# Two attention blocks on one core: the first x and K loads copied plain and transposed by TensorE

## The chip, the cores and the metric

One core of one Trainium2 chip. The metric is the device time of one execution in microseconds; lower is better. Before the change it is 1212.87 us, the median of three runs (1212.12 to 1215.04).

## What is computed

Two independent attention blocks, A and B, of the same shape, whose outputs stand side by side in the last dimension:

```python
# x 16x144x448, k_cache and v_cache 16x16x512x256, wq 448x4096, wo 4096x448, all bf16
q = (x @ wq).reshape(B, Sq, H, Dh).transpose(0, 2, 1, 3)
scores = jnp.einsum("bhqd,bhkd->bhqk", q, k_cache) * (Dh ** -0.5)
p = softmax(scores, axis=-1)
o = jnp.einsum("bhqk,bhkd->bhqd", p, v_cache)
out = o.transpose(0, 2, 1, 3).reshape(B, Sq, H * Dh) @ wo
# result: concatenate([out of A, out of B], axis=-1), 16x144x896
```

## The kernel before

The work is cut into 512 **units** (`NT`): 2 blocks x 16 batches x 16 heads, A first. A unit is 144 query rows against 512 keys of depth 256. Line numbers are those of the profile.

Every buffer is allocated by hand, and the program of each engine is written by one loop over **slots** `i`. In a slot each step is emitted for the unit that is due there: Q for unit `i + LQ` (15 ahead), SA for `i + LS` (5 ahead), TA for `i + LT` (2 ahead), PV for `i`. A small bookkeeper (`_Sched.add`) turns the reads and writes of each step into semaphore waits; each engine then executes its own list strictly in order. Nothing is reordered at run time.

The steps of a unit:

- **Q** (`t_q`, L316): 8 matmuls 128x144 into the one bank `qp_ps`; evacuated with the factor 1/16 into `qt_sb` by VectorE (L328) or ScalarE (L332).
- **SA** (`t_sa`, L424): scores of the first 112 query rows, 2 matmuls 128x512 into one of two banks `sa_ps`; then maximum on VectorE (L436), exponential on ScalarE (L447), reciprocal on VectorE (L457), normalisation on GpSimd (L465).
- **SB** (`t_sb`, L348): scores of the last 32 rows of 8 units together, 16 matmuls into two banks `sb_ps`; once in 8 slots, in slot 8n - 7 for group n. It needs the whole K block of the group and the Q of its 8 units.
- **TA** and **TB** (L478, L401): the probabilities transposed by TensorE, 4 transposes each, evacuated by VectorE (L488, L410).
- **PV** (`t_pv`, L511): 8 matmuls into one of two banks `ot_ps`; evacuated by ScalarE (L526) into a ring that collects batches.
- **OP** (`t_op_piece`, L549): output projection of finished chunks of 128 rows with `wo`, in pieces of 2 matmuls between the other steps, from slot 17 on. Evacuated at L567 (ScalarE) or L570 (VectorE), and stored by GpSimd's queue (`t_store`, L578). The last two chunks end in the banks `op_ps` and `qp_ps`.

**Loads.** All go through SP's queue, in an order that is sorted beforehand by deadline (`plan`: a deadline, an earliest slot `lo` and a lead). x comes for four batches at a time by two DMA transposes (L281, L282; `xt_sb`, three buffers). K comes for 8 units at a time by one DMA transpose (L291; `kt_sb`, three buffers): K0 is the block of units 0 to 7, K1 of 8 to 15, and so on. V comes for 4 units at a time as a plain copy (L301; `v_sb`, three buffers; V0 for units 0 to 3). wq comes in four parts for four heads each, two copies a part (L260, L262): wq0 for units 0 to 3, and so on. wo comes in 8 parts of 448 KB (L270). A load into a buffer waits on SP for the last reader of what lay there.

The order on SP's queue at the start of the kernel before is x, wq0, wq1, wq2, K0, wq3, V0, K1, V1, V2, K2, wo, V3, 2 wo, V4, K3, 2 wo, V5, 2 wo, V6, K4, wo, V7, V8, K5.

Of the kernel before, what the change touches and what calls it, by code (L numbers as in the profile page):

```python
# [122 lines left out]
def bass_concat_heads__mha_block_cached__gqa_block_cached__near_ridge_kernel(  # L123
# [52 lines left out]
    with contextlib.ExitStack() as es:  # L176
# [126 lines left out]

        def t_q(U):
# [4 lines left out]
            hg = h // 4  # L309

            def e(t):
                ins = None
                for kc in range(4):
                    for dc in range(2):
                        c0 = h * DH + dc * 128
                        ins = t.matmul(qp_ps[:, dc * SQ:(dc + 1) * SQ], lhsT=wq_sb[:, kc, c0:c0 + 128],  # L316
# [3 lines left out]
            S.add(PE, e, reads=[(("wq", hg), pr), ("wqz", 0), (("xt", xsl), XG)], writes=[("qp", ("q", U))],  # L320
                  banks=["qp"], name="Q%d" % U)

        def t_evac_q(U):
            sl = U % NQT
            src = qp_ps[:, 0:2 * SQ].rearrange("p (c q) -> p c q", c=2)
            if (U - LQ) % 8 in (2, 4, 6, 7):
                def e(v):
                    return v.tensor_scalar(qt_sb[:, sl, :, :], src, 1.0 / 16.0, None, op0=ALU.mult)  # L328
                S.add(DVE, e, reads=[("qp", ("q", U))], writes=[(("qt", sl), U)], banks=["qp"], name="eq%d" % U)
            else:  # L330
                def e(a):
                    return a.activation(qt_sb[:, sl, :, :], src, AF.Copy, scale=1.0 / 16.0)  # L332
# [240 lines left out]
        def t_store(r):  # L573
            pr, row0, m = chunk_rows(r)
            sl = r % NOST

            def e(q):
                return q.dma_start(of[row0:row0 + m, pr * D:(pr + 1) * D], ost_sb[0:m, sl, :]).then_inc(  # L578
                    sems["ost%d" % sl], 16)
# [228 lines left out]
```

## Time and profile before

| | before |
|---|---|
| time, median of 3 runs | 1212.87 us (1212.12 to 1215.04) |
| the profiled execution | 1210.82 us, span 1209.1 us |
| TensorE busy | 1174.4 us, 97% |
| VectorE, ScalarE, GpSimd busy | 770.1, 753.7, 678.5 us |
| TensorE, ScalarE, VectorE first used for units | 10.33, 11.48, 13.13 us |
| first PV | 37.88 us |
| issue to landing, K transposes | median 15.2 us (11.4 to 20.2) |
| DMA moved | 294.15 MB, mean 243 GB/s |

The profile is one execution on the chip. The span runs from the first to the last event of the core; the executions' times are 1.7 us or so longer. "Busy" is the time in which an engine executes something. In a row of the timeline stand the start, the length, the engine, the line, the operation, output and input, the number of instructions merged, and in brackets the idle time before the first of them, with what ended it. "SPq" is the time in which SP's sequencer works on issuing a transfer, which is not the transfer itself.

### The profile page before, as it was taken

What the parts mean: (1) busy time and instruction counts of PE and PEld (TensorE: products, weight loads), DVE (VectorE), ACT (ScalarE), POOL (GpSimd) and SP (SyncE); (2) the same over time, 40 slices, a digit from 0 to 9 for tenths busy, and PEclk for the clock granted to TensorE, in tenths of its full rate; (3) what the DMA queues carried; (4) which work ended last, traced back from release to release, by engine and by line L of the source; (5) the groups of instructions that cost most, each with busy time, mean ns of one, the idle gap of its engine ahead of it and who ended that gap; (6) DMA issues with size and microseconds to landing.
All of it is one profiled execution on the core that took longest, in us unless ns stands there. A gap on an engine that the chain in (4) does not pass through costs nothing.

```text
span 1209.1 us, 33868 instructions
## 1 busy us (share of the span) xinstructions
PE 1174.4 (97%) x13952; PEld 894.2 (74%) x13952; DVE 770.1 (64%) x2179; ACT 753.7 (62%) x2213; POOL 678.5 (56%) x682
## 2 busy tenths in 40 slices
PE   4898999999999999999999999999999999999997
PEld 3676777777777777777777777777777777777765
DVE  1765666666666666666666666666666666666563
ACT  1665666666666666666666666666666666666553
POOL 0555565565555565565555655655655655665553
PEclk9999999999999999999999999999999999999999
DMA  9999999999999999999999999998999999999971
GB/s 249 281 285 289 245 252 225 245 251 247 246 235 237 231 259 226 246 246 232 290 283 282 284 272 265 228 258 225 245 244 236 224 249 244 242 240 234 232 178 47
DMA packets 627033, 294.15 MB, mean 243 GB/s; under 512 B 548416, under 2 KB 556608, under 8 KB 626880
## 3 DMA queue, kind: packets, MB, share of 16 engines
q1 hardware_dynamic: 625152, 287.85, 101.8%
q0 software_dynamic: 1728, 4.13, 1.1%
q8 instruction: 111, 1.82, 0.6%
q14 instruction: 42, 0.34, 0.1%
HBM read 148.90 MB, written 4.13 MB: 127 GB/s over the span
## 4 chain that ended last, share of the span: by engine, by line
PE 90%; DMA 5%; DVE 3%; SPq 1%; ACT 0%; issue 0%; POOL 0%; ACTq 0%
PE qp_ps L316 20%; PE ot_ps L511 19%; PE sa_ps L424 19%; PE op_ps L549 17%; PE sa_ps L478 8%; PE sb_ps L348 5%; DMA kt_sb<-in_A_k_cache_dram 3%; PE sb_ps L401 2%; DMA kt_sb<-in_B_k_cache_dram 2%; DVE stat L436 1%; DMA wq_sb<-in_A_wq_dram 0%; DVE pt_sb L488 0%; PE qp_ps L549 0%; DVE pt_sb L410 0%; DVE qt_sb L328 0%
## 5 line engine op out<-in xcount | busy, mean ns | idle before, releaser
L465 POOL TENSOR_TENSOR pa_sb<-pa_sb,stat 112x512 bf16<-112x512 bf16 x512 | 531.8, 1039 | 490.8 <-DVE stat L457 490.7
L447 ACT ACTIVATE pa_sb<-sa_ps,stat 112x512 bf16<-112x512 f32 x512 | 352.1, 688 | 408.0 <-DVE stat L436 407.0
L436 DVE TENSOR_REDUCE stat<-sa_ps 112x1 f32<-112x512 f32 x512 | 353.9, 691 | 324.6 <-PE sa_ps L424 321.1
L316 PE MATMUL qp_ps<-xt_sb,wq_sb 128*128 128x144 bf16 x4096 | 344.1, 228 | 16.1 <-DMA wq_sb<-in_A_wq_dram 10.3
L316 PEld LDWEIGHTS qp_ps<-xt_sb,wq_sb 128*128 128x128 bf16 x4096 | 290.5, 99 | 93.1 <-issue 11.1
L511 PE MATMUL ot_ps<-pt_sb,v_sb 128*128 128x144 bf16 x4096 | 340.4, 226 | 0.0
L424 PE MATMUL sa_ps<-kt_sb,qt_sb 128*112 128x512 bf16 x1024 | 310.9, 385 | 1.0 <-DVE pt_sb L488 0.8
L549 PE MATMUL op_ps<-wo_sb,ring 128*128 128x448 bf16 x1120 | 278.8, 352 | 0.0
L511 PEld LDWEIGHTS ot_ps<-pt_sb,v_sb 128*128 128x128 bf16 x4096 | 268.5, 97 | 0.4
L478 PEld LDWEIGHTS sa_ps<-ident,pa_sb 112*128 112x128 bf16 x2048 | 145.0, 97 | 111.3 <-ACT pa_sb L447 24.9
L526 ACT ACTIVATE ring<-ot_ps 128x288 bf16<-128x288 f32 (+8 forms) x512 | 190.3, 372 | 4.4 <-PE ot_ps L511 4.4
L488 DVE COPY pt_sb<-sa_ps 128x448 bf16<-128x448 bf16 x512 | 190.7, 372 | 2.4 <-PE sa_ps L478 2.4
L478 PE MATMUL sa_ps<-ident,pa_sb 112*128 112x112 bf16 x2048 | 185.4, 212 | 0.1
L328 DVE TENSOR_SCALAR qt_sb<-qp_ps 128x288 bf16<-128x288 f32 x256 | 117.0, 457 | 96.5 <-PE qp_ps L316 93.9
L389 POOL TENSOR_TENSOR pb_sb<-pb_sb,stat 128x512 bf16<-128x512 bf16 x128 | 132.8, 1037 | 27.1 <-DVE stat L381 27.1
L332 ACT ACTIVATE qt_sb<-qp_ps 128x288 bf16<-128x288 f32 x256 | 106.0, 414 | 35.0 <-PE qp_ps L316 32.5
L424 PEld LDWEIGHTS sa_ps<-kt_sb,qt_sb 128*112 128x112 bf16 x1024 | 97.0, 129 | 38.8 <-issue 26.7
L549 PEld LDWEIGHTS op_ps<-wo_sb,ring 128*128 128x128 bf16 x1120 | 95.1, 98 | 27.6 <-ACT ring L526 0.2
L447 ACT ACTIVATION_READ_ACCUMULATOR pa_sb<-sa_ps,stat 112x1 f32 x512 | 98.9, 193 | 0.0
L361 DVE TENSOR_REDUCE stat<-sb_ps 128x1 f32<-128x512 f32 x128 | 87.2, 681 | 3.7 <-PE sb_ps L348 3.7
L371 ACT ACTIVATE pb_sb<-sb_ps,stat 128x512 bf16<-128x512 f32 x128 | 88.5, 691 | 0.0
L457 DVE RECIPROCAL stat<-stat 112x1 f32<-112x1 f32 x512 | 78.4, 153 | 0.5 <-ACT pa_sb L447 0.5
(23 smaller groups left out, 366.1 us busy)
## 6 DMA issues: line engine op xcount, KB each, us to landing
v_sb<-in_A_v_cache_dram SPq DMA_DIRECT2D x64, 1024.0 KB, 6.1
v_sb<-in_B_v_cache_dram SPq DMA_DIRECT2D x64, 1024.0 KB, 6.0
out_dram<-ost_sb POOLq DMA_DIRECT2D x36, 112.0 KB, 5.1
wo_sb<-in_A_wo_dram SPq DMA_DIRECT2D x8, 448.0 KB, 6.3
wo_sb<-in_B_wo_dram SPq DMA_DIRECT2D x8, 448.0 KB, 6.2
wq_sb<-in_A_wq_dram SPq DMA_DIRECT2D x4, 768.0 KB, 6.7
wq_sb<-in_B_wq_dram SPq DMA_DIRECT2D x4, 768.0 KB, 7.6
wq_sb<-in_A_wq_dram SPq DMA_DIRECT2D x4, 128.0 KB, 6.9
```

The source lines that it names most:

```text
L316: ins = t.matmul(qp_ps[:, dc * SQ:(dc + 1) * SQ], lhsT=wq_sb[:, kc, c0:c0 + 128], rhs=xt_sb[:, xsl, kc, xo:xo + SQ], start=(kc == 0 and dc ...
L328: return v.tensor_scalar(qt_sb[:, sl, :, :], src, 1.0 / 16.0, None, op0=ALU.mult)
L389: return g.tensor_tensor(pb_sb[:, psl, :], pb_sb[:, psl, :], stat[:, RINVB + sl:RINVB + sl + 1].to_broadcast([128, SK]), op=ALU.mult)
L424: ins = t.matmul(sa_ps[bank][0:QA, :].rearrange("q (k r) -> q k r", k=KR), lhsT=qt_sb[:, U % NQT, dc, 0:QA], rhs=kt_of(U, dc), start=(dc = ...
L436: return v.tensor_reduce(stat[0:QA, NEG + sl:NEG + sl + 1], sa_ps[bank][0:QA, :], axis=AX.X, op=ALU.max, negate=True)
L447: return a.activation(pa_sb[0:QA, psl, :], sa_ps[bank][0:QA, :], AF.Exp, bias=stat[0:QA, NEG + sl:NEG + sl + 1], scale=1.0, accum_out=stat ...
L465: return g.tensor_tensor(pa_sb[0:QA, psl, :], pa_sb[0:QA, psl, :], stat[0:QA, RINV + sl:RINV + sl + 1].to_broadcast([QA, SK]), op=ALU.mult)
L478: ins = t.transpose(pta_ps[bank][:, c * 128:c * 128 + QA], src[:, c, :], ident[0:QA, 0:QA])
L488: return v.tensor_copy(pt_sb[:, sl, :, 0:QA], pta_ps[bank][:, 0:512].rearrange("p (c q) -> p c q", c=4)[:, :, 0:QA])
L511: ins = t.matmul(ot_ps[ob][:, dc * SQ:(dc + 1) * SQ], lhsT=v_sb[:, vsl, j, c * DH + dc * 128:c * DH + (dc + 1) * 128], rhs=pt_sb[:, sl, c, ...
L526: ins = a.activation(ring[:, 2 * h:2 * h + 2, c0:c0 + n1], src[:, :, 0:n1], AF.Copy)
L549: ins = t.matmul(acc[0:m, 0:D], lhsT=ring[:, c, col0:col0 + m], rhs=wo_sb[:, c, :], start=(c == first), stop=(c == last))
```

## The change

It concerns the first 16 units, and the last two stores.

- **x of the first four batches** is copied untransposed (`t_load_x_nat`), in two copies, into a part of `wo_sb` that isn't needed yet. TensorE transposes it in three steps (`t_xt`, 20 transposes into `sb_ps` and one `sa_ps` bank), evacuated by VectorE, ScalarE and VectorE.
- **K0 and K1** are copied untransposed in four halves of 4 units (`t_load_k_nat`, kn0 to kn3, with the access pattern of a V load): kn0 and kn1 into the third K buffer, kn2 and kn3 into `wo_sb`. TensorE transposes them unit by unit (`t_kt`, 8 transposes each, KT0 to KT15), evacuated into the K buffers by VectorE for even units and ScalarE for odd ones. The first DMA transpose on the queue is that of K2. It waits for KT7; the first wo load waits for KT15 and the x transposes.
- **The order of the start is written out.** Q of units 0 to 15 alternates between two banks (`q_bank`). Q0 to Q3 and KT0 to KT3 come in slot -7, Q4 to Q7 and KT4 to KT7 in -6, Q8, Q9, SB0 and SA0 in -5, Q10 and Q11 in -4, KT8 to KT11 in -3 and -2, Q12 and Q13 in -1, Q14 and Q15 in 0, KT12 to KT15 in 1 and 2, SB1 and Q16 in 3. Q16 to Q23 share slots 3 to 8. From slot 9 (SB2) on the order is the one of before.
- **Warm-up matmuls**: 10 matmuls 128x512 on zeros ahead of the x transposes and 6 behind them (`t_warm`), into a bank that is not read.
- **The order on SP's queue** at the start becomes x (2 copies), wq0, kn0, wq1, kn1, wq2, kn2, V0, wq3, kn3, V1, V2, K2, 4 wo, V3, V4, K3, V5, 4 wo, V6, K4, V7, V8, K5; after that it is as before.
- **The stores of the last two chunks** are issued by SP instead of GpSimd, each with a semaphore of its own; SP waits for both at its end.

The core of the diff:

```diff
+    NKT = 16
+    N_WARM = (10, 6)
...
+        kt0_nat = kt_sb[:, 2].rearrange("p k d r -> p (k d r)").rearrange("p (u c e) -> p u c e", u=8, c=4)
+        wo_flat = wo_sb[:].rearrange("p c e -> p (c e)")
+        kt1_nat = wo_flat[:, 0:8 * 4 * DH].rearrange("p (u c e) -> p u c e", u=8, c=4)
+        x_nat = wo_flat[:, 8 * 4 * DH:8 * 4 * DH + 5 * D].rearrange("p (t e) -> p t e", t=5)
...
+        def t_load_x_nat():
+            x = xs[0][0:XB].rearrange("b q d -> (b q) d")
+            nf = XB * SQ // 128
+
+            def e(q):
+                q.dma_start(x_nat[:, 0:nf, :], x[0:nf * 128, :].rearrange("(t p) d -> p t d", p=128)).then_inc(
+                    sems["xn"], 16)
+                return q.dma_start(x_nat[0:XB * SQ - nf * 128, nf, :], x[nf * 128:XB * SQ, :]).then_inc(sems["xn"], 16)
...
+        def t_load_k_nat(hf):
+            pr, b, h0 = unit(4 * hf)
+            src = ks[pr][b, h0:h0 + 4].rearrange("u (p c) d -> p u (c d)", p=128)
+            dst = kt_nat[hf // 2][:, 4 * (hf % 2):4 * (hf % 2) + 4].rearrange("p u c e -> p u (c e)")
...
+        def t_xt(k):
...
+                for r0 in range(0, n, 128):
+                    m = min(128, n - r0)
+                    for kc in range(4):
+                        c0 = min(128 * kc, D - 128)
+                        ins = t.transpose(dst[:, kc, r0:r0 + m], x_nat[0:m, 2 * k + r0 // 128, c0:c0 + 128],
+                                          ident[0:m, 0:m])
...
+        def t_kt(u):
+            ot = ((("otp", u % 2), "ot%d" % (u % 2), ot_ps[u % 2].bitcast(BF16)))
+            key, bank, acc = ot if u < 12 else ((("sbb", 0), "sb0", ptb_ps[0]) if u % 2 else
+                                                ("opp", "op", op_ps.bitcast(BF16)))
...
+                for c in range(KR):
+                    for dc in range(2):
+                        ins = t.transpose(acc[:, (2 * c + dc) * 128:(2 * c + dc + 1) * 128],
+                                          kt_nat[u // 8][:, u % 8, c, dc * 128:(dc + 1) * 128], ident[:, :])
...
+            eng = ACT if u % 2 else DVE
...
+            w = [(("kn", 0), 1), (("kn", 1), 1)] if SG == 2 else []
...
+        def q_bank(U):
+            return (op_ps, "opp", "op") if U < 16 and U % 2 else (qp_ps, "qp", "qp")
...
+        def t_warm(k):
+            def e(t):
+                ins = None
+                for _ in range(N_WARM[k]):
+                    ins = t.matmul(sa_ps[1][:, :], lhsT=ident[:, :], rhs=pt_sb[:, 0, :, 0:128], start=True, stop=True)
+                return ins
...
-            S.add(POOL, e, reads=[(("ost", sl), r)], dma_sem="ost%d" % sl, name="st%d" % r)
+            S.add(SP if r in tail_chunks else POOL, e, reads=[(("ost", sl), r)], dma_sem=sem, name="st%d" % r)
...
+        sb_slot = [8 * n - LSB for n in range(NSG)]
+        sb_slot[0:2] = [-LS, 3]
+        q_slot = [u - LQ for u in range(NT)]
+        q_slot[0:24] = [-7] * 4 + [-6] * 4 + [-5, -5, -4, -4, -1, -1, 0, 0] + [3, 4, 4, 5, 6, 6, 7, 8]
+        kt_slot = [-7] * 4 + [-6] * 4 + [-3, -3, -2, -2, 1, 1, 2, 2]
...
-                dl = pr * NU + 4 * hg - LQ
+                dl = pr * NU + 4 * hg - LQ if pr > 0 else (-59, -57, -55, -52)[hg]
...
+        plan(s_min, -60, 0, t_load_x_nat)
+        for hf in range(4):
+            plan(s_min, (-58, -56, -54, -51)[hf], 0, t_load_k_nat, hf)
         for wg in range(NWG):
-            plan(s_min, H - 4 + 2 * wg, 10 ** 6, t_load_wo, 0, wg)
-        for SG in range(NSG):
-            dl = 8 * SG - LSB
+            plan(3, 4 if wg < 4 else 9.5, 10 ** 6, t_load_wo, 0, wg)
+        for SG in range(2, NSG):
+            dl = {2: 2, 3: 8.5}.get(SG, 8 * SG - LSB)
...
-            dl = 4 * G
+            dl = (-53, -50, -49, 5, 6, 9)[G] if G < 6 else 4 * G
...
+            if i == q_slot[0]:
+                t_warm(0)
+                for k in range(3):
+                    t_xt(k)
+                t_warm(1)
+            for u in q_at.get(i, ()):
                 t_q(u)
                 t_evac_q(u)
+            for n in sbs.get(i, ()):
+                t_sb(n)
...
+            for u in kt_at.get(i, ()):
+                t_kt(u)
```

More of the change, by code (lines that the diff above doesn't have):

```diff
@@ L238, in t_ident, with t_warm_zero, e @@
             S.add(POOL, e2, reads=[("ones", 0)], writes=[("ident", 0)], name="ident")
+        def t_warm_zero():
+            def e(v):
+                return v.memset(pt_sb[:, 0, :, :], 0.0)
+            S.add(DVE, e, writes=[("warm", 0)], name="warmz")
         def t_wqzero():
@@ L309, in t_q @@
             hg = h // 4
+            acc, key, bank = q_bank(U)
             def e(t):
@@ L328, in e @@
                     return v.tensor_scalar(qt_sb[:, sl, :, :], src, 1.0 / 16.0, None, op0=ALU.mult)
-                S.add(DVE, e, reads=[("qp", ("q", U))], writes=[(("qt", sl), U)], banks=["qp"], name="eq%d" % U)
+                S.add(DVE, e, reads=[(key, ("q", U))], writes=[(("qt", sl), U)], banks=[bank], name="eq%d" % U)
             else:
@@ L332, in e @@
                     return a.activation(qt_sb[:, sl, :, :], src, AF.Copy, scale=1.0 / 16.0)
-                S.add(ACT, e, reads=[("qp", ("q", U))], writes=[(("qt", sl), U)], banks=["qp"], name="eq%d" % U)
+                S.add(ACT, e, reads=[(key, ("q", U))], writes=[(("qt", sl), U)], banks=[bank], name="eq%d" % U)
         def kt_of(U, dc):
@@ L765, in body @@
                         ins.then_inc(sems[eng_name], 1)
+                if eng_name == SP:
+                    for k in range(len(tail_chunks)):
+                        eng.wait_ge(sems["ostt%d" % k], 16)
                 if eng_name == POOL:
```

115 lines of the change are left out of this document (73 added, 42 removed).

## The prediction

> **What bounds the kernel now.** I read the page's busy shares and chain first, then TensorE's waits over the whole span, then the timelines of TensorE and of SP's queue up to 135 us, last the DMA rate by stage.
>
> ```profile
> PE 1174.4 (97%) x13952; PEld 894.2 (74%) x13952; DVE 770.1 (64%) x2179; ACT 753.7 (62%) x2213; POOL 678.5 (56%) x682
> PE 90%; DMA 5%; DVE 3%; SPq 1%; ACT 0%; issue 0%; POOL 0%; ACTq 0%
> ```
>
> TensorE is busy for 1174.4 of 1209.1 us. Not one of the 512 units loses work by the change, so what can be won is the 34.7 us in which TensorE is idle, and work that it does slowly. Its waits name the places:
>
> ```profile
> PE qp_ps L316 <- DMA wq_sb<-in_A_wq_dram: 10.3, 1, 10.3
> PE sb_ps L348 <- DMA kt_sb<-in_A_k_cache_dram: 6.1, 4, 1.9
> PE qp_ps L316 <- DVE qt_sb L328: 3.1, 6, 0.6
> PE sb_ps L348 <- DMA kt_sb<-in_B_k_cache_dram: 2.9, 2, 2.2
> ```
>
> There are 10.3 us before the first matmul, 3.1 us of Q behind its own evacuation, 6.1 us before four scores of K of problem A, and 2.9 us at the change to problem B. The timeline (start, length, line) shows where the first three lie:
>
> ```profile
> 10.33 1.12 PE L316 MATMUL qp_ps<-xt_sb,wq_sb 128*128 128x144 bf16 x8 [10.33 <-DMA wq_sb<-in_A_wq_dram]
> ...
> 23.69 1.90 PE L348 MATMUL sb_ps<-kt_sb,qt_sb 128*32 128x512 bf16 x16 [0.54 <-ACT qt_sb L332]
> ...
> 27.16 0.67 PE L316 MATMUL qp_ps<-xt_sb,wq_sb 128*128 128x144 bf16 x8 [0.51 <-ACT qt_sb L332]
> ...
> 37.88 0.66 PE L511 MATMUL ot_ps<-pt_sb,v_sb 128*128 128x144 bf16 x8
> ...
> 56.49 1.05 PE L348 MATMUL sb_ps<-kt_sb,qt_sb 128*32 128x512 bf16 x16 [1.60 <-DMA kt_sb<-in_A_k_cache_dram]
> ...
> 73.76 1.05 PE L348 MATMUL sb_ps<-kt_sb,qt_sb 128*32 128x512 bf16 x16 [1.48 <-DMA kt_sb<-in_A_k_cache_dram]
> ...
> 94.47 1.05 PE L348 MATMUL sb_ps<-kt_sb,qt_sb 128*32 128x512 bf16 x16 [1.10 <-DMA kt_sb<-in_A_k_cache_dram]
> ...
> 112.87 1.05 PE L348 MATMUL sb_ps<-kt_sb,qt_sb 128*32 128x512 bf16 x16 [1.93 <-DMA kt_sb<-in_A_k_cache_dram]
> ...
> 132.41 1.05 PE L348 MATMUL sb_ps<-kt_sb,qt_sb 128*32 128x512 bf16 x16
> ```
>
> The first PV starts at 37.88. SB2, SB3, SB4 and SB5 then each wait for K (1.60, 1.48, 1.10, 1.93); SB6 at 132.41 waits for nothing. So up to 112.87 the kernel is held by the transfers, and behind that by TensorE. SP's queue says the same:
>
> ```profile
> 7.34 14.10 SPq L291 DMA_TRANSPOSE kt_sb<-in_A_k_cache_dram  x1
> ...
> 23.27 13.47 SPq L291 DMA_TRANSPOSE kt_sb<-in_A_k_cache_dram  x1
> ...
> 37.96 14.40 SPq L291 DMA_TRANSPOSE kt_sb<-in_A_k_cache_dram  x1
> 52.41 0.58 SPq L270 DMA_DIRECT2D wo_sb<-in_A_wo_dram  x1
> ...
> 56.80 14.78 SPq L291 DMA_TRANSPOSE kt_sb<-in_A_k_cache_dram  x1
> ```
>
> Each transpose of K holds SP about 14 us, and what follows is issued at its end (37.96 + 14.40 is followed by wo at 52.41). Up to the last of these rows SP is never without something to issue, so what counts is how long the transfers take. The windows view by stage (the last column is GB/s) prices them:
>
> ```profile
> 4.00:15.00 11.00, 3.40 (x24) 2.55 (x24) 0.46 (x1) 0.59 (x2) 0.00 (x0) 1.00 0.97 261
> 15.00:23.50 8.50, 5.71 (x40) 4.25 (x40) 1.37 (x3) 0.95 (x3) 0.00 (x0) 1.00 1.26 258
> 23.50:30.00 6.50, 5.18 (x49) 2.94 (x50) 1.68 (x4) 1.60 (x5) 1.04 (x1) 1.00 1.18 311
> 30.00:38.40 8.40, 6.66 (x75) 4.53 (x73) 6.64 (x20) 5.18 (x15) 5.08 (x5) 1.00 1.14 248
> 38.40:44.80 6.40, 6.26 (x83) 4.39 (x81) 4.02 (x13) 4.50 (x13) 3.36 (x4) 1.00 1.13 331
> ...
> 56.40:64.00 7.60, 7.43 (x95) 5.36 (x96) 5.20 (x15) 4.56 (x13) 4.07 (x4) 1.00 1.17 374
> ```
>
> 4 to 15 is wq0 to wq2; 15 to 23.5 is K0, 30 to 38.4 K1, both by DMA transpose; 23.5 to 30 is wq3 and V0; 38.4 to 44.8 is V1 and V2; 56.4 to 64 is wo and V. A block of K is 8 x 512 x 256 x 2 bytes, 2.10 MB, the same as two loads of V.
>
> **The change part by part.**
>
> *K0 and K1 as copies.* The transposes take 8.5 and 8.4 us. The copies have the access pattern of V. At the V1, V2 row (331) 2.10 MB take 6.3 us, at the quickest plain row (374) 5.6, at the slowest (261) 8.0. The saving is 16.9 - 12.6 = 4.3 us, bounds 0.9 and 5.7. I take 331, as the same pattern into the same memory.
>
> *wq0 to wq2* stay copies, 2.75 MB in 11 us at 261. Copies now stand between them, and no transpose behind them. Bounds: nothing won, or 2.7 us at 331. I take half, 1.3. x goes from transposes to copies of the same 0.5 MB: nothing, give or take 1. So the transfers from V2 on run 4.3 + 1.3 = **5.6 us earlier** (bounds 0.9 and 8.4). One wo load (448 KB, 1.2 us at 374) moves ahead of K3 from behind K4: the lead is 4.4 at K3 and K4, 5.6 again at K5.
>
> [...]
>
> *TensorE's path to the first PV.* It now waits for data in the order x, wq0, K half 0, wq1, K half 1, wq2, K half 2, V0, wq3. Q12, the first that needs wq3, stands in slot -1. Up to wq3 there are 0.5 MB of x and 7.9 MB behind it. From 4.0 (x in) at 300 GB/s, between 261 and 331, wq3 lands at 30.2 (34.1 and 27.8 by the ends). Durations of steady steps, from the chain:
>
> ```profile
> 45.12 0.50 PE qp_ps L316 x8
> 45.62 0.58 PE sa_ps L424 x2
> 46.20 0.20 PE sa_ps L478 x4
> 46.40 0.22 PE sb_ps L401 x4
> 46.63 0.50 PE ot_ps L511 x8
> ```
>
> Before wq3, TensorE has 12 Q (6.0 us), 12 K units of 8 transposes (2 x 0.22 each, 5.3), SB0 (1.05) and four SA (2.3): 14.7 us in the 21 from wq0 on, so that is covered. After wq3 come four Q, two SA, two TA and a TB: 2.0 + 1.16 + 0.40 + 0.22 = 3.8, and PV0 starts at 34.0, **3.9 us ahead of 37.88**. Then KT12 to KT15 in slots 1 and 2 add 4 x 0.44 = 1.8. By slot 9 both kernels have done the same 24 Q. TensorE is 2.1 ahead, and if all four K waits went (6.1), it would be **8.2 ahead** at SB5.
>
> *Which of the two holds.* SB2 is wanted at 56.49 - 1.60 - 2.1 = 52.8, K2 lands at 56.4 - 5.6 = 50.8. (A K block lands about 0.1 before the SB that waited for it starts.) SB3 is wanted 15.8 later (56.49 to 73.76 less the wait), at 68.6; K3 lands at 73.6 - 4.4 = 69.2. SB4 is wanted at 69.2 + 19.6 = 88.8, K4 lands at 94.3 - 4.4 = 89.9. SB5 is wanted at 89.9 + 16.5 = 106.4, K5 lands at 112.7 - 5.6 = 107.1. The transfers hold; the gain is **5.6 us**, with K waits of about 0.6, 1.1 and 0.7 left.
>
> *Evacuations.* K's are 128 x 1024, even units on VectorE, odd on ScalarE. The nearest rows are the page's group of VectorE copies of 448 columns, and the costliest-groups view of the last 20 us:
>
> ```profile
> L488 DVE COPY pt_sb<-sa_ps 128x448 bf16<-128x448 bf16 x512 | 190.7, 372 | 2.4 <-PE sa_ps L478 2.4
> ```
>
> ```profile
> L567 ACT ACTIVATE ost_sb<-op_ps 128x448 bf16<-128x448 f32 x1 | 0.5, 544 | 0.8 <-PE op_ps L549 0.8
> ```
>
> Scaled by 1024/448 the ends are 0.85 and 1.24 us. Four units in two banks then take about 3 us; four of them stand behind each half of K, which arrives every 6 us or so with its wq. In slots 1 and 2 they add 2.5 us to ScalarE; there TensorE may lose up to 2 us, of the 8.2 - 5.6 = 2.6 to spare. Cost nothing; if that cover is gone, up to 2.
>
> *Waits on SP.* K2's transpose waits for KT7, since the copies lie in its buffer: about 21 us, with V0, wq3, K and V queued in front until 39. The wo loads wait for KT15, at about 38, behind K2's 14 us. Both are past when their turn comes. The 16 warm-up matmuls run while x and wq0 are on their way: nothing.
>
> *The last two stores.*
>
> ```profile
> 1202.25 0.54 ACT L567 ACTIVATE ost_sb<-op_ps 128x448 bf16<-128x448 f32 x1 [0.78 <-PE op_ps L549]
> 1202.64 0.62 DVE L570 CAST ost_sb<-qp_ps 128x448 bf16<-128x448 f32 x1 [4.21 <-PE qp_ps L549]
> 1203.09 1.12 POOL L578 DMA_DIRECT2D out_dram<-ost_sb  x2 [7.06 <-ACT ost_sb L567]
> ```
>
> ```profile
> out_dram<-ost_sb POOLq DMA_DIRECT2D x2, 112.0 KB, 1.9
> ```
>
> POOL issues both in 1.12 us from 1203.09, landing 1.9 us after issue. SP needs about 0.58 us an issue (the wo row at 52.41) and can begin at 1202.8, but its second waits for the cast until 1203.26, and its latency on an empty queue is not shown. Bounds: 1 us won, 1 lost; I take 0.
>
> **Sum.** The profiled execution took 1210.82 (span 1209.1 and 1.7 around it). 1210.82 - 5.6 = 1205.2. The median of the runs shown is 2.05 above that execution, so 1212.87 - 5.6 = **1207.3 us**.
>
> **Rivals.**
>
> 1. *Copies no faster than transposes* (the 261 row for all of K): lead about 1, time about 1211.9. For: the first copies of the kernel run at 261. Against: 331 and 374 later.
>
> 2. *TensorE stays slow until the SB0 burst.* The Q groups from 10.33 take 1.12 to 1.16 us and SB0 1.90, from 27.16 on 0.67 and 1.05, although the clock column says 1.00 throughout. Here the warm-up matmuls ought to bring the change forward. If not, and Q0 starts at 9.5, ten Q at 1.14, eight K units at twice 0.44 and SB0 at 1.9 end at 30; two Q, four SA, four K units, a TA and a TB (5.5) and the 3.8 above then lead to PV0 at 39.3: 37.88 - 39.3 - 1.8 + 6.1 = 2.9 ahead, about 1210.0. [...]
>
> 3. *Slower: TensorE slow all the way to the first PV.* With no burst long enough, from 9.5 on 12 Q at 1.14, 12 K units at 0.88, SB0 at 1.9, four SA at 1.16 and the last stretch at twice 3.8 end at 47.8, 9.9 behind PV0 now; with 1.8 of K, and 6.1 of waits gone, 5.6 slower, 1218.5. It decides from PV0 at 37.88 + 6.1 - 1.8 = 42.2 on. Against: 21 us for 14.7 of work.
>
> 4. *All copies at 331 to 374*: transfers 8.4 or more ahead and wq3 sooner, so TensorE's 8.2 to 10 hold: about 1204.
>
> **How the numbers follow.** Chances: forecast 0.58, rival 1 0.10, rival 2 0.08, rival 3 0.09, rival 4 0.15. A difference under 0.3% (3.6 us) can't be told from none here. Forecast and rival 4 are faster by more: 0.73; rivals 1 and 2 are within it: 0.18; rival 3 is slower: 0.09. The range 1202.5 to 1211.0 takes in the forecast with its bounds, rival 4 and rival 2, and leaves out rivals 3 and 1, about 0.19.
>
> **What would show it.** Right: PV0 near 34; K2's data from about 39; the waits of SB3 to SB5 near 1 us or gone; SB5 near 107; SB6 and all behind it, the 2.9 us at problem B among it, as before, only earlier; K copies near 331 GB/s. Wrong: Q groups of 1.14 us behind the warm-up, K copies under 270 GB/s, a stretch in slots 1 to 8 that ScalarE ends, or new waits behind 135 us. The end wrong: more than 1 us between the last evacuation and the end gained or lost.

## The result, and the profile after

The changed kernel takes **1207.47 us** (median of 10 executions, 1204.72 to 1211.09) against 1213.16 us of the kernel before beside it (10 executions, 1211.82 to 1215.04). The ratio is 0.9954, 95% interval 0.9940 to 0.9969: 5.6 us less, between 3.8 and 7.3. The profiled execution took 1205.52 us, its span is 1203.8 us, 5.3 less than before. One execution of e4 below (1233.95 us, at a granted clock of 0.944 where all others have 0.99 or more) was in a slower state of the chip and is left out of its range and ratio.

TensorE's waits over the whole span (us in total, times, longest):

```profile
PE sb_ps L440 <- DMA kt_sb<-in_B_k_cache_dram: 3.5, 3, 1.7
PE qp_ps L398 <- DMA wq_sb<-in_A_wq_dram: 3.0, 3, 1.4
PE sb_ps L440 <- DMA kt_sb<-in_A_k_cache_dram: 1.8, 2, 1.1
PE qp_ps L398 <- ACT qt_sb L415: 1.7, 1, 1.7
```

The 10.3 us before the first Q are now work (the warm-up matmuls and the transposes of x) and short waits. A's waits for K have fallen from 6.1 to 1.8 us, but B's have grown from 2.9 to 3.5, and there is a new one of 1.7 for an evacuation. Where they stand, from TensorE's timeline:

```profile
9.69 0.66 PE L398 MATMUL qp_ps<-xt_sb,wq_sb 128*128 128x144 bf16 x8 [0.84 <-DMA wq_sb<-in_A_wq_dram]
...
34.90 0.66 PE L603 MATMUL ot_ps<-pt_sb,v_sb 128*128 128x144 bf16 x8
...
41.26 1.05 PE L440 MATMUL sb_ps<-kt_sb,qt_sb 128*32 128x512 bf16 x16 [0.71 <-ACT kt_sb L359]
...
44.98 0.67 PE L398 MATMUL qp_ps<-xt_sb,wq_sb 128*128 128x144 bf16 x8 [0.91 <-DVE qt_sb L411]
...
50.73 0.67 PE L398 MATMUL qp_ps<-xt_sb,wq_sb 128*128 128x144 bf16 x8 [1.67 <-ACT qt_sb L415]
...
56.95 1.05 PE L440 MATMUL sb_ps<-kt_sb,qt_sb 128*32 128x512 bf16 x16
...
128.36 1.05 PE L440 MATMUL sb_ps<-kt_sb,qt_sb 128*32 128x512 bf16 x16
...
289.81 1.05 PE L440 MATMUL sb_ps<-kt_sb,qt_sb 128*32 128x512 bf16 x16 [0.74 <-DMA kt_sb<-in_A_k_cache_dram]
...
581.15 1.05 PE L440 MATMUL sb_ps<-kt_sb,qt_sb 128*32 128x512 bf16 x16 [1.10 <-DMA kt_sb<-in_A_k_cache_dram]
601.70 1.05 PE L440 MATMUL sb_ps<-kt_sb,qt_sb 128*32 128x512 bf16 x16 [1.70 <-DMA kt_sb<-in_B_k_cache_dram]
619.39 1.05 PE L440 MATMUL sb_ps<-kt_sb,qt_sb 128*32 128x512 bf16 x16 [0.67 <-DMA kt_sb<-in_B_k_cache_dram]
...
730.81 1.05 PE L440 MATMUL sb_ps<-kt_sb,qt_sb 128*32 128x512 bf16 x16 [1.18 <-DMA kt_sb<-in_B_k_cache_dram]
```

The rows are Q0, PV0, SB1, Q18, Q21, SB2, SB6, and then SB15, SB31, SB32, SB33 and SB39. SB1, Q18 and Q21 wait for evacuations, SB2 to SB6 for nothing. Set against the start of the same SB in the kernel before:

| | SB2 | SB5 | SB6 | SB15 | SB31 | SB32 | SB33 | SB39 | SB63 |
|---|---|---|---|---|---|---|---|---|---|
| before, us | 56.49 | 112.87 | 132.41 | 293.20 | 583.51 | 604.55 | 622.30 | 732.47 | 1168.01 |
| after, us | 56.95 | 108.82 | 128.36 | 289.81 | 581.15 | 601.70 | 619.39 | 730.81 | 1166.30 |
| lead of after | -0.46 | 4.05 | 4.05 | 3.39 | 2.36 | 2.85 | 2.91 | 1.66 | 1.71 |

So 4.05 us are won by SB6, and on balance 2.34 of them are lost again at K blocks far behind, SB15, SB31 and SB39, where the kernel before waits for nothing. TensorE ends only 1.7 us earlier. The rest of the 5.3 us lies behind its last matmul, in the timeline of the end:

```profile
1200.28 0.54 PE L641 MATMUL qp_ps<-wo_sb,ring 128*128 128x448 bf16 x2
...
1201.11 0.83 SPq L671 DMA_DIRECT2D out_dram<-ost_sb  x2
```

From the end of the last matmul (1200.82) to the end of the span (1203.8) it takes 3.0 us. Before, the last matmul ended at 1202.53 and the span at 1209.1: 6.6 us. That is 3.6 us; 1.7 + 3.6 = 5.3.

### The profile page after: what moved, and what is told of

It reads as the page before. It is cut to its first block, busy times and chain, and to the rows that moved or that the text cites. A ratio compares the mean times of both kernels' runs of the same rounds, so it can differ in the third digit from the quotient of the medians.

```text
span 1203.8 us, 34217 instructions
## 1 busy us (share of the span) xinstructions
PE 1183.8 (98%) x14116; PEld 901.8 (75%) x14116; DVE 776.3 (64%) x2190; ACT 762.2 (63%) x2222; POOL 678.4 (56%) x680
## 4 chain that ended last, share of the span: by engine, by line
PE 88%; DMA 6%; DVE 3%; SPq 3%; ACT 0%; issue 0%; POOL 0%; DVEq 0%
PE ot_ps L603 19%; PE sa_ps L516 18%; PE qp_ps L398 18%; PE op_ps L641 17%; PE sa_ps L570 8%; PE sb_ps L440 5%; DMA kt_sb<-in_B_k_cache_dram 3%; DMA kt_sb<-in_A_k_cache_dram 2%; PE sb_ps L493 2%; DVE stat L528 1%; SPq L294 1%; DMA wq_sb<-in_A_wq_dram 1%; SPq L295 1%; PE qp_ps L641 0%; DVE pt_sb L580 0%; SPq L272 0%
## 5 line engine op out<-in xcount | busy, mean ns | idle before, releaser
L398 PEld LDWEIGHTS qp_ps<-xt_sb,wq_sb 128*128 128x128 bf16 x4032 | 283.3, 98 | 80.0 <-DMA wq_sb<-in_A_wq_dram 2.6
L398 PE MATMUL qp_ps<-xt_sb,wq_sb 128*128 128x144 bf16 x4032 | 334.5, 226 | 5.6 <-DMA wq_sb<-in_A_wq_dram 3.0
L411 DVE TENSOR_SCALAR qt_sb<-qp_ps 128x288 bf16<-128x288 f32 x250 | 114.1, 457 | 79.4 <-PE qp_ps L398 78.5
```

The source lines that it names most:

```text
L398: ins = t.matmul(acc[:, dc * SQ:(dc + 1) * SQ], lhsT=wq_sb[:, kc, c0:c0 + 128], rhs=xt_sb[:, xsl, kc, xo:xo + SQ], start=(kc == 0 and dc = ...
```

## The experiments

Each was timed beside the kernel before on the same chip. The leads are those of the profiled execution's SB6 and SB63 over the kernel before, in us; "end" is the time from the end of the last matmul to the end of the span.

| | what differs | time, us | ratio to before (95%) | SB6 | SB63 | end |
|---|---|---|---|---|---|---|
| after | | 1207.47 | 0.9954 (0.9940 to 0.9969) | 4.05 | 1.71 | 3.0 |
| e1_tail_only | before, with the stores on SP | 1211.02 | 0.9978 (0.9968 to 0.9987) | -0.65 | -1.00 | 3.0 |
| e2_front_only | after, with the stores on GpSimd | 1210.71 | 0.9974 (0.9964 to 0.9985) | 2.96 | -0.82 | 6.6 |
| e3_two_banks | after, second bank for Q up to Q23 | 1207.28 | 0.9950 (0.9934 to 0.9965) | 5.72 | 3.33 | 3.0 |
| e4_k_transposed | after, with K0 and K1 by DMA transposes | 1215.19 | 1.0009 (0.9995 to 1.0022) | -0.98 | -4.41 | 3.0 |
| e5_no_warm | after, without the warm-up | 1205.86 | 0.9939 (0.9922 to 0.9955) | 4.45 | 1.97 | 2.9 |
| e6_x_transposed | after, with the first x by DMA transposes | 1207.27 | 0.9943 (0.9930 to 0.9956) | 3.39 | -0.85 | 3.0 |
| e7_x_split | after, with later x loads in two parts, earlier | 1202.74 | 0.9906 (0.9892 to 0.9921) | 2.54 | 3.00 | 3.0 |
| e8_tail_mixed | after, with one of the two stores on GpSimd | 1209.04 | 0.9968 (0.9956 to 0.9981) | 3.74 | -1.64 | 4.4 |
| e9_combined | e3 and e7 together | 1202.97 | 0.9905 (0.9890 to 0.9921) | 4.82 | 3.07 | 2.9 |
| e10_k_tail_split | e7 without x copies and warm-up | 1203.32 | 0.9925 (0.9912 to 0.9938) | 3.22 | 3.46 | 2.9 |

The profiled executions differ for the same work: e8 and e2 have the front and the loads of the changed kernel, with 3.74 and 2.96 at SB6, and from SB6 to SB63 they lost 5.38 and 3.78 us where the changed kernel's lost 2.34. So the leads of one trace tell where something goes, and the ratio how much it is worth.

### The two halves apart: stores alone, front alone

```diff
# e1_tail_only: the kernel before, with
-            S.add(POOL, e, reads=[(("ost", sl), r)], dma_sem="ost%d" % sl, name="st%d" % r)
+            S.add(SP if r in tail_chunks else POOL, e, reads=[(("ost", sl), r)], dma_sem=sem, name="st%d" % r)
# e2_front_only: the changed kernel, with
-            S.add(SP if r in tail_chunks else POOL, e, reads=[(("ost", sl), r)], dma_sem=sem, name="st%d" % r)
+            S.add(POOL, e, reads=[(("ost", sl), r)], dma_sem=sem, name="st%d" % r)
```

> The kernel before with one edit: the last two stores on SP's queue, with SP waiting for them. Theory (the store path sets 3.6 us of the end): up to the last matmul all is as before; the span ends 3.0 us after the last matmul (after: 1200.82 to 1203.8) instead of 6.6 (before: 1202.53 to 1209.1), so about 3.6 us faster than before, near 1209.5. Rival (the end of the changed kernel is short for another reason, such as what GpSimd or SP did earlier): the end stays 6 us or more behind the last matmul, no difference from before.

> The changed kernel with its last two stores back on GpSimd's queue. Theory: the front alone. The first part as in the changed kernel (SB6 near 128.4, 4 us ahead of before), the end 6.6 us behind the last matmul again, so about 3.6 us slower than the changed kernel, 1.5 to 4 us faster than before, near 1210.5, the spread coming from K waits behind x loads. Rival (the front gives the whole 5.6 us and the stores nothing): as fast as the changed kernel, near 1207.5.

The stores alone give -2.7 us (-1.6 to -3.9), the front alone -3.2 (-1.8 to -4.4); together -5.9, next to -5.6 of the whole. In the profile of e1 the end is 3.0 us, though its TensorE ended a microsecond later than in the kernel before; in e2 it is 6.6. The timeline of the end of e1, then of e2:

```profile
1202.98 0.54 PE L549 MATMUL qp_ps<-wo_sb,ring 128*128 128x448 bf16 x2
...
1203.81 0.83 SPq L579 DMA_DIRECT2D out_dram<-ost_sb  x2
```

```profile
1202.81 0.54 PE L641 MATMUL qp_ps<-wo_sb,ring 128*128 128x448 bf16 x2
...
1203.91 1.11 POOL L671 DMA_DIRECT2D out_dram<-ost_sb  x2 [7.05 <-ACT ost_sb L659]
```

e1's span ends at 1206.5, 2.7 us behind the first issue, as in the changed kernel (1201.11 to 1203.8). e2's ends at 1209.9, 6.0 behind, as in the kernel before (1203.09 to 1209.1). So about half of the gain is the place of two stores. In e2's profiled execution the whole lead of the front, 2.96 us, is gone by the end; there SB31 alone waits 2.8 us for K.

### Is it the copies of K?

```diff
...
-            w = [(("kn", 0), 1), (("kn", 1), 1)] if SG == 2 else []
+            w = []
...
-        for u in range(NKT):
-            at(kt_at, kt_slot[u], u)
...
-        for hf in range(4):
-            plan(s_min, (-58, -56, -54, -51)[hf], 0, t_load_k_nat, hf)
+        for SG in range(2):
+            plan(s_min, (-54, -51)[SG], 0, t_load_k, SG)
```

> The changed kernel with K0 and K1 by DMA transpose again (behind wq2 and behind wq3), without the 128 transposes on TensorE; x, the order of Q, the warm-up and the stores as in the changed kernel. Theory (the gain of the front is the transfers' lead, 2 x 2.1 us of it from K): K0 lands near 21, PV0 starts early, near 31, but K2 lands near 54 instead of 49, and SB2 to SB5 wait for K again, 5 us or so in all; SB6 is 1 to 2.7 us ahead of before instead of 4.05, so 1.5 to 3 us slower than the changed kernel. Rival (the earlier start of TensorE is what counts): SB6 at least 4 us ahead of before, as fast as the changed kernel or faster.

The whole front gain goes, and more: 1215.19 us (1210.76 to 1219.35). By the ratio that is 1.1 us above the kernel before, with an interval that includes no difference, although its stores are on SP. Three rows of TensorE's timeline:

```profile
24.17 1.90 PE L440 MATMUL sb_ps<-kt_sb,qt_sb 128*32 128x512 bf16 x16 [7.22 <-DMA kt_sb<-in_A_k_cache_dram]
...
26.89 1.16 PE L398 MATMUL qp_ps<-xt_sb,wq_sb 128*128 128x144 bf16 x8
...
76.18 1.69 PE L440 MATMUL sb_ps<-kt_sb,qt_sb 128*32 128x512 bf16 x16 [4.09 <-DMA kt_sb<-in_A_k_cache_dram]
```

SB0 waits 7.22 us for K0. Behind that wait everything takes twice as long (SB0 1.90 instead of 1.05, Q 1.16 instead of 0.66), and again behind the 4.09 us of SB3. I had expected 1 to 2.7 us ahead at SB6 and found 0.98 behind. The slow stretch behind SB3, which I had not counted, is 1.6 us of that. More of it is K3: it lands at 76.06, 2.5 us later than in the kernel before (73.60), although K2 lands 0.4 earlier. In e4 one more wo load stands ahead of K3 (1.2 us by the prediction's price); the rest is not explained. So e4 shows that the front's gain goes without the K copies, but not cleanly how much of the 6.7 us between it and the changed kernel, by the ratios, is their transfer alone.

The windows view (the last three columns are the granted clock, DMA share and GB/s) shows both the clock and the rate, the stage of K0 in e4 first and two stages of the changed kernel behind it:

```profile
16.00:24.00 8.00, 0.94 (x16) 0.76 (x13) 0.46 (x1) 0.41 (x1) 0.00 (x0) 0.65 1.29 236
```

```profile
9.70:15.70 6.00, 4.71 (x65) 3.77 (x66) 2.30 (x4) 2.57 (x4) 0.00 (x0) 1.00 1.06 330
15.70:22.70 7.00, 4.69 (x65) 3.74 (x66) 2.30 (x4) 3.17 (x5) 0.00 (x0) 1.00 1.05 347
```

With K0 as a transpose the stage has 236 GB/s, with copies 330 and 347. The 236 are an average of two things. The DMA view of e4 from 15.3 to 24.0, in slices of 0.22 us:

```profile
GB/s 168 291 290 291 290 290 292 288 291 290 292 290 292 287 291 291 290 348 272 53 0 2 8 9 9 149 287 294 287 288 294 286 294 287 292 291 288 350 160 122
```

While K0 is transposed the engines move 290 GB/s, very evenly, and in between there are 1.3 us in which they move next to nothing. The kernel before shows the same rate for K1 from 31.5 us on (287 to 293 GB/s), and a similar hole right ahead of it (19 to 50 GB/s from 30.1 to 31.5). What causes the hole the trace does not show. K2, the first transpose that both have, lands at 55.98 in e4 and at 48.96 in the changed kernel: by that, the copies of the two blocks are worth 7.0 us of transfer time.

### What the warm-up and the copies of x carry

```diff
# e5_no_warm
-                t_warm(0)
...
-                t_warm(1)
# e6_x_transposed
...
-            if XG:
-                plan(lo, dl, 40, t_load_x, XG)
+            plan(lo, dl if XG else -60, 40, t_load_x, XG)
...
-        plan(s_min, -60, 0, t_load_x_nat)
...
-                for k in range(3):
-                    t_xt(k)
```

> The changed kernel without its two warm-up calls (10 units of four matmuls ahead of the x transposes, 6 behind them); nothing else differs. Theory (the warm-up units are what puts TensorE at full speed before slot 0): without them the Q groups run at about 1.1 us instead of 0.66 and the K units at about 0.88 instead of about 0.66, up to the first S block; the first PV starts near 39 us instead of 34.9; by the sixth S block the run is 0.5 to 1 us ahead of the kernel before instead of 4.05, and the whole is about 3.5 us longer than the changed kernel. Rival (the Q groups, which are long enough, release the clock themselves within their first group or two): below 1 us longer, the first PV within 1 us of 34.9.

> The changed kernel with x of the first four batches loaded by DMA transposes again, so that TensorE's x transposes are gone; K's first 16 units stay copied. Theory (K's copies carry the front's gain, x's copies none of it): the first Q group starts about 10.3 us instead of 9.69, the first PV within 1 us of 34.9, the whole within 1 us of the changed kernel. Rival (x's copies matter because a transposed x load holds the queues against the K copies behind it): the first PV 2 us or more later, and the whole 2 us or more longer.

Without the warm-up the first matmuls are indeed slow, but nothing follows from it. The timeline of e5:

```profile
9.43 1.12 PE L398 MATMUL qp_ps<-xt_sb,wq_sb 128*128 128x144 bf16 x8 [2.44 <-DMA wq_sb<-in_A_wq_dram]
...
12.26 1.17 PE L398 MATMUL op_ps<-xt_sb,wq_sb 128*128 128x144 bf16 x8
...
15.06 0.62 PE L349 MATMUL ot_ps<-ident,kt_sb 128*128 128x128 bf16 x8 [0.19 <-DVE kt_sb L359]
...
34.47 0.66 PE L603 MATMUL ot_ps<-pt_sb,v_sb 128*128 128x144 bf16 x8
```

Four Q groups run at about half speed, then TensorE is fast by itself. They and the K transposes right behind them lose some 2 us, in a stretch in which the changed kernel waits for wq anyway; PV0 is at 34.47 (34.90 with the warm-up), and the time is 1205.86, not longer. My theory of the warm-up fell. (The warm-up is 10 and 6 matmuls, not units of four as I wrote there.) The copies of x are worth nothing either: in e6 Q0 starts at 10.45 instead of 9.69, PV0 at 35.54, and the time is 1207.27.

### Which wait held the front: two banks for Q

```diff
-            return (op_ps, "opp", "op") if U < 16 and U % 2 else (qp_ps, "qp", "qp")
+            return (op_ps, "opp", "op") if U < 24 and U % 2 else (qp_ps, "qp", "qp")
```

> The changed kernel with Q of units 16 to 23 alternating between the two banks as well (the limit 16 in q_bank becomes 24). Theory (TensorE lost time in slots 1 to 8 because two Q of one slot share one bank): the waits of 0.91 us at 44.98 and 1.67 us at 50.73 go, SB2 starts near 54.4 instead of 56.95; K4 and K5, landing near 90.3 and 107.5, hold then, so SB5 starts near 107.6 instead of 108.82: 1.2 us faster than the changed kernel. Rival (the evacuations of K on ScalarE and VectorE themselves are too much for slots 1 to 8): SB2 stays at 56.5 or later and nothing is won.

Slots 4 and 6 of the changed kernel hold two Q each, both into the one bank `qp_ps`. The second (Q18, Q21) waits until VectorE or ScalarE, which have other work queued ahead, has emptied the bank of the first: the 0.91 and 1.67 us. With two banks both waits are gone, and SB2 (54.95) and SB5 (107.15) start 2.0 and 1.7 us earlier than in the changed kernel. The K waits of e3's timeline up to SB39, without the two of SB32 and SB33:

```profile
90.62 1.05 PE L440 MATMUL sb_ps<-kt_sb,qt_sb 128*32 128x512 bf16 x16 [0.23 <-DMA kt_sb<-in_A_k_cache_dram]
...
579.30 1.05 PE L440 MATMUL sb_ps<-kt_sb,qt_sb 128*32 128x512 bf16 x16 [1.56 <-DMA kt_sb<-in_A_k_cache_dram]
...
729.16 1.05 PE L440 MATMUL sb_ps<-kt_sb,qt_sb 128*32 128x512 bf16 x16 [1.71 <-DMA kt_sb<-in_B_k_cache_dram]
```

SB4 waits 0.2 us, so from there on the transfers hold. The lead at SB6 is 5.72 us. But SB31 and SB39 then wait 1.56 and 1.71 instead of 1.10 and 1.18: who comes earlier waits longer. In the timing the two kernels can't be told apart.

### Why the later K blocks are late: the x loads

In the changed kernel SP's timeline has, ahead of SB39:

```profile
708.82 6.00 SPq L294 DMA_TRANSPOSE xt_sb<-in_B_x_dram  x1
714.87 3.26 SPq L295 DMA_TRANSPOSE xt_sb<-in_B_x_dram  x1
718.17 9.66 SPq L368 DMA_TRANSPOSE kt_sb<-in_B_k_cache_dram  x1
```

The x load of four batches holds SP for 9.3 us right ahead of K39, which so is issued at 718.17 and lands 0.14 us before its SB at 730.81. In the kernel before the same x load held SP for 5.4 us, and K39 was issued at 717.24, earlier than here although all else is later there. Why the load takes longer here the trace does not show. K15 stands behind an x load in the same way, K31 behind one and a part of B's wq.

```diff
...
-                plan(lo, dl, 40, t_load_x, XG)
+                early = 24 if XG > 1 else 0
+                plan(lo, dl - early - 8.5, 40, t_load_x, XG, 0)
+                plan(lo, dl - early, 40, t_load_x, XG, 1)
```

The numbers in `plan` are slots, of about 2.3 us each; the expectation calls them us. The edit does two things at once: it splits each load, and from the third x group on it issues both parts 24 slots or more earlier.

> The changed kernel with each later x load split into its two parts, planned apart: the first part of group 1 8.5 us ahead of its due time and the second at it, those of the later groups 32.5 and 24 us ahead instead of both together. Theory (an x load standing in one piece ahead of a K block on the same queue pushes that K late, and takes back 2.35 us of the 4.05 gained at the front): the waits at the S blocks 15, 31 and 39 (0.74, 1.10 and 1.18 us) vanish, those at 32 and 33 (no x load, wq of the second half) stay; TensorE ends 2 to 3 us earlier than in the changed kernel, the whole near 1205. Rival (the K blocks are late for another reason): the waits stay or move to other K blocks, and the time is that of the changed kernel within 0.5 us.

> The changed kernel with both edits: the second bank for Q kept up to unit 24 instead of 16, and the later x loads split into two parts planned apart. Theory: the gains of the front (about 1.6 us more at the sixth S block) and of the later K blocks (2 to 3 us) add, and the whole ends near 1203.5, 3.5 to 4.5 us ahead of the changed kernel. Rival (one wait takes the place of the other: a front that is earlier makes the same K blocks late by as much): no more than the better of the two alone.

e7 takes 1202.74 us (1200.88 to 1204.22), with an interval (0.9892 to 0.9921) that lies wholly below that of the changed kernel: the largest step of the study. The changed kernel was timed on another chip; e5 and e6, which the timing can't tell from it, were timed beside e7 and took 1205.86 and 1207.27. K39 is now issued at 708.75, and TensorE waits for K at SB32, SB33 (0.24 us) and SB37 only; the timeline of SB32, SB37 and SB39:

```profile
600.59 1.05 PE L441 MATMUL sb_ps<-kt_sb,qt_sb 128*32 128x512 bf16 x16 [0.76 <-DMA kt_sb<-in_B_k_cache_dram]
...
693.32 1.05 PE L441 MATMUL sb_ps<-kt_sb,qt_sb 128*32 128x512 bf16 x16 [1.39 <-DMA kt_sb<-in_B_k_cache_dram]
...
729.49 1.05 PE L441 MATMUL sb_ps<-kt_sb,qt_sb 128*32 128x512 bf16 x16
```

The waits of SB15, SB31 and SB39 are gone. That at SB15 proves little, as only the changed kernel's own trace has it. But of the six kernels with the new front and unsplit x loads (after, e2, e3, e5, e6, e8), five wait at SB31 and five at SB39; of the three with split loads (e7, e9, e10) none does, e9 not even with a lead of 4.82 us at SB31. A wait of 1.39 us has come up at SB37. K37 stands behind five loads of B's wo, in the changed kernel too, where it landed 1.02 us before its SB; here TensorE wants it 1.5 us earlier and it lands 0.8 later. From SB6 to SB63 e7 wins 0.46 us on the kernel before, where the changed kernel lost 2.34: the 2.8 us that the theory gave. The profiled execution shows less at the end (TensorE 1.3 us earlier than in the changed kernel): its lead at SB6 is 2.54 us, where the changed kernel's is 4.05, with a wait of 1.68 us for wq at 22.78 ahead of it. The timing shows more. So it is shown that the x loads ahead of K31 and K39 were the cause; the exact size is not, nor whether the splitting or the earlier issue does it.

e9 fell short: 1202.97 us, no better than e7 alone. Its lead is 7.18 us at SB33, and then one wait takes more than half of it (timeline, SB37 and SB38):

```profile
691.61 1.05 PE L441 MATMUL sb_ps<-kt_sb,qt_sb 128*32 128x512 bf16 x16 [2.42 <-DMA kt_sb<-in_B_k_cache_dram]
...
711.03 1.05 PE L441 MATMUL sb_ps<-kt_sb,qt_sb 128*32 128x512 bf16 x16
```

The wait costs 2.42 us and TensorE at half speed behind it 1.7 more: SB37 to SB38 takes 19.42 us here and 17.76 in the kernel before. The rival held: between 577 and 727 us, where the loads for problem B pile up on SP's queue, the transfers set the pace. Four kernels that go in with leads of 2.5 to 5.7 us at SB6 (e3, e7, e9, e10) all come out of it with 3.0 to 3.5.

### Only what carries the gain

e10 is e7 with the two edits of e5 and e6 as well.

> The kernel with the split x loads, with x of the first four batches loaded by DMA transposes and without both warm-up calls: of the change only K's 16 copied units, the first DMA transpose at K2, and the last two stores on SP are left. Theory (these, with the split, carry the whole gain; the x copies, TensorE's x transposes and the warm-up carry none): the first Q groups run at half speed (1.17 us) from about 10.4 us on, the sixth S block starts 2.5 to 3.5 us ahead of the kernel before, and the whole is within 1 us of the kernel with the split alone, 1202.74. Rival (each start spoiled costs its own share to the end): the first PV starts 36 us or later, and the whole is 1.5 us or more longer than with the split alone.

1203.32 us (1202.67 to 1205.02). The first Q groups take 1.12 to 1.16 us, PV0 stands at 35.71, SB6 3.22 us ahead: all as expected. By the medians it is 0.6 us from e7, but the two were timed on different chips; by the ratios to the kernel before it is 2.3 us longer. The intervals of the ratios (0.9912 to 0.9938 and 0.9892 to 0.9921) overlap at their edge. So the rival, 1.5 us or more, isn't excluded. Taken out of the changed kernel one at a time (e5, e6), the warm-up and the copies of x were worth nothing that the timing shows; whether both together are worth a microsecond or two stays open.

### What the stores cost on GpSimd's queue

```diff
-            S.add(SP if r in tail_chunks else POOL, e, reads=[(("ost", sl), r)], dma_sem=sem, name="st%d" % r)
+            S.add(SP if r == tail_chunks[-1] else POOL, e, reads=[(("ost", sl), r)], dma_sem=sem, name="st%d" % r)
```

> The changed kernel with the first of the last two out-stores back on GpSimd's queue and the second left on SP's; SP waits for both. Theory (what ends the run late is the completion of a store that GpSimd issued, which comes some 3 us after its data have landed, while that of an SP store comes within 1 us): with one such store left the span still ends about 6 us behind the last matmul, as in the kernel before (6.6), and the run is 2 to 3 us longer than the changed kernel. Rival (the two stores cost because GpSimd issues them one behind the other, 1.12 us in all, or because GpSimd itself ends late): the span ends 3 to 3.6 us behind the last matmul, and the run is within 1 us of the changed kernel.

Neither held. The end is 4.4 us, between the 3.0 of two SP stores and the 6.6 of two GpSimd stores, and the run takes 1209.04 us; by the ratios it is 1.7 us longer than the changed kernel, with intervals that overlap. The timeline of its end:

```profile
1203.63 0.54 PE L641 MATMUL qp_ps<-wo_sb,ring 128*128 128x448 bf16 x2
...
1204.73 0.58 POOL L671 DMA_DIRECT2D out_dram<-ost_sb  x1 [7.05 <-ACT ost_sb L659]
1204.93 0.36 SPq L671 DMA_DIRECT2D out_dram<-ost_sb  x1
```

From GpSimd's issue (1204.73) to the end of the span (1208.6) it takes 3.9 us with one store, 6.0 with two. So both halves of my two theories are in it: the last store of GpSimd ends late, and a second one behind it adds 2.1 us, four times the 0.56 that issuing it takes. The GB/s rows of the DMA view, cut into 40 slices, show the data; first before from 1203.0 on (slices of 0.15 us), then after from 1200.5 on (0.08 us), then e8 from 1204.0 on (0.115 us):

```profile
GB/s 0 0 0 0 0 0 0 0 411 270 71 206 300 247 0 0 0 0 0 0 0 0 0 0 0 0 0 0 0 0 0 0 0 0 0 0 0 0 0 0
```

```profile
GB/s 0 0 0 0 0 0 0 0 0 0 0 0 0 0 0 0 0 43 239 369 358 304 76 54 250 337 391 294 66 0 0 0 0 0 0 0 0 0 0 0
```

```profile
GB/s 0 0 0 0 0 0 0 0 0 0 0 0 0 0 0 62 335 374 639 304 234 47 0 0 0 0 0 0 0 0 0 0 0 0 0 0 0 0 0 0
```

Each row ends with the span. The data are all moved 4.0 us before the end with two GpSimd stores, 2.1 with one, 0.9 with none. What fills that time the trace does not show.

## Why the prediction came out, step by step

The number was right, 1207.3 against 1207.47, and so was the sign. But its one term, 5.6 us from transfers, isn't what happened. The 5.3 us between the two profiles are 4.05 from the front, -2.34 given back behind it, and 3.6 from the stores: the front fell short by 1.6 and 2.3 were given back, and the stores, put at nothing, made up for it. That the number fits is luck. Point by point:

**The transfers: right, and a little better than said.** SP's timeline and the DMA view of the changed kernel (last column: us from issue to landing) give the K blocks; the rows are those of K2 and K5:

```profile
26.76 19.54 SPq L368 DMA_TRANSPOSE kt_sb<-in_A_k_cache_dram  x1
...
89.70 13.41 SPq L368 DMA_TRANSPOSE kt_sb<-in_A_k_cache_dram  x1
```

```profile
kt_sb<-in_A_k_cache_dram SPq DMA_TRANSPOSE x1, 22.2
...
kt_sb<-in_A_k_cache_dram SPq DMA_TRANSPOSE x1, 17.8
```

| lands at | K2 | K3 | K4 | K5 |
|---|---|---|---|---|
| forecast | 50.8 | 69.2 | 89.9 | 107.1 |
| after | 48.96 | 69.24 | 90.30 | 107.50 |

The copies moved at 330 to 347 GB/s, next to the 331 that was taken. K2's turn on SP came at 26.76, not "until 39"; it then sat 19.54 us in the issue, so it landed 1.8 us ahead of the forecast and no more. How the lead is made up was off: by e4 the two K blocks bring 7.0 of the 7.4 us by which K2 landed earlier, where the sum had 4.3 for K (5.7 at most) and 1.3 for wq. Where the other 2.7 of K come from is not taken apart here. Behind the wo loads the lead was 4.4 at K3, 4.0 at K4 and 5.2 at K5, near the 4.4, 4.4 and 5.6 that were said.

**Rival 1 did not occur.** It had the copies no faster than the transposes. e4 against the changed kernel shows them faster here: 290 GB/s while K0 is transposed and 236 over its stage, 330 to 347 with copies, and 7.0 us at the landing of K2.

**"Which of the two holds" is the step that failed.** The prediction had SB2 wanted at 52.8 and the transfers behind it in charge. SB2 started at 56.95, 4.15 us later, without waiting for K, which had landed 8 us before. The 4.15 are four rows: PV0 0.9 later than said (34.90 against 34.0), then 0.71 at SB1, 0.91 at Q18 and 1.67 at Q21; 4.19 in all. So in this stretch TensorE set the pace, and its lead is made of the K waits that went (1.48 + 1.10 + 1.93 at SB3 to SB5) less the 0.46 by which SB2 was late: 4.05. The prediction had named the mechanism, a stretch in slots 1 to 8 that ScalarE ends, and had given it 2 us out of a cover of 2.6. Taken that way the four rows, 4.2 us, overran the cover by 1.6, and 5.6 - 1.6 = 4.0. e3, which takes away the two largest of the rows, gives 5.72 at SB6.

What it missed is where the wait arises. It looked at the evacuations of K, which are quicker than it said (0.69 and 1.02 us, forecast 0.85 and 1.24), and not at the Q of slots 3 to 8, two to a slot on one bank.

**"Everything behind SB6 as before" failed as well.** It holds for the work, not for the waits. K blocks that came just in time before come late when TensorE is 4 us ahead, as the transfers around an x load have no 4 us to give: in the changed kernel's trace they cost 0.69 at SB15, 1.06 at SB31, 1.25 at SB39. B's two waits (2.19 and 0.72 before, 1.70 and 0.67 after) shrank by 0.54 in all. A look at the slack of each K block in the trace before, its landing against its SB, would have shown two of them: 1.31 us at SB15 and 0.21 at SB31, while a usual block has 4 to 7. It would also have named K7 (0.52), which then did not come late. K39 had 3.83, and the longer x load ahead of it took up the rest.

**The last two stores were priced at 0, within 1 us either way. They gave 3.6 in the profile and 2.7 timed** (1.6 to 3.9). The prediction looked at when the data land, where there is little to win, and not at how long the span goes on behind the landing. The rows of before held it: landing 1.9 us after issue, data done by 1205.1, end of the span 1209.1.

**Rivals 2 and 3 did not occur, and the reason given against rival 2, the warm-up, was not the right one.** The warm-up did put TensorE at full speed for Q0 (0.66 us at 9.69), but e5 shows that it comes to speed by itself within 5.6 us (9.43 to 15.06), under cover of the transfers. The condition of rival 3, PV0 behind 42.2, is far off. But a slow TensorE does cost time where it is not covered: e4 loses 1.6 us to it behind SB3.

## What to carry to other kernels

A lead won at the front of a kernel that runs at 97% of its bound is kept only as far as the transfers behind it have slack (here 1.71 of 4.05 us were left at SB63): list for every later load when it lands and when it is wanted, before adding up. Where the lead is given back, look at what is issued just ahead of the late load; taking that apart and issuing it earlier (the x loads here) brought as much again as the whole change (0.9906 of the kernel before instead of 0.9954). And read the end of a span separately: what lies between the last data and the last event belongs to the time as well, and a queue can be chosen for it (here 3.0 us behind the last matmul with both stores on SP's, 6.6 with both on GpSimd's).

## What the hardware did that was not expected

**A wait of TensorE can cost more than its length.** Behind some long waits TensorE works at about half speed for some 3 us or more (in e2 behind SB31 from 584.8 to 588.3, with a PV of 1.17 us instead of 0.67), and the clock column of the windows view is below 1.00 there (0.69 in e2 from 583.3 to 587.3, 0.65 in e9 from 691.5 to 695.5). It does not show everything: the first Q groups of the kernel before take 1.12 to 1.16 us instead of 0.67, with 1.00 in the column from 10.33 to 23.5. Three K waits at the same place, SB32, in the timelines of e5, e6 and e1:

```profile
601.75 1.90 PE L440 MATMUL sb_ps<-kt_sb,qt_sb 128*32 128x512 bf16 x16 [2.25 <-DMA kt_sb<-in_B_k_cache_dram]
```

```profile
601.80 1.90 PE L440 MATMUL sb_ps<-kt_sb,qt_sb 128*32 128x512 bf16 x16 [2.83 <-DMA kt_sb<-in_B_k_cache_dram]
```

```profile
606.25 1.05 PE L348 MATMUL sb_ps<-kt_sb,qt_sb 128*32 128x512 bf16 x16 [3.25 <-DMA kt_sb<-in_B_k_cache_dram]
```

Behind 2.25 and 2.83 us SB32 takes 1.90 instead of 1.05; behind 3.25 us it does not. Between SB32 and SB33 the kernel before takes 17.75 us, 0.72 of them wait; e5 takes 18.58 and e6 19.92 without a wait: 1.6 and 2.9 us lost on top. From SB2 on, no wait up to 2.19 us (before, SB32) was followed by a loss. Of the longer ones 2.42 (e9), 2.75 (e4), 2.83 (e2), 3.22 (e8) and 4.09 (e4) each lost 1.4 to 1.7 us on top, but 2.48 (e1, SB5) lost nothing, like the 3.25 above. So in these runs the length of the wait alone does not tell whether it happens: 2.42 us did it, 2.48 and 3.25 did not. What else decides the traces do not show.

Such losses would also explain why the splitting of the x loads did more in the timing than in the profile: in all nine executions of e7 and e10 the mean granted clock is 0.999 or 1.000, in four of the ten of the changed kernel 0.997, and 0.003 of 1204 us is 3.6 us. But e9, as fast as e7, has 0.997 and 0.998 in two of its four. As those executions have no profile, this is argued and not shown.

**With a store on GpSimd's queue at the very end the span goes on for 2 to 4 us behind the last data** (4.0 with two such stores, 2.1 with one), with SP's stores alone for 0.9.
